# Loading every K and V tile as two column halves, one through the SyncE queue and one through the ScalarE queue

## The chip, the cores and the metric

The kernel runs on one core of one Trainium2 chip. The metric is the time of one execution in microseconds of device time. A time in this document is the median of a kernel's runs. Where a kernel was timed, its runs took turns with runs of the kernel before on the same chip. The kernel before had 1334.65 us (three runs, 1334.62 to 1334.92).

## The reference

The kernel computes one decode step of attention over a long cache, next to a small gated MLP mixer. Only the attention matters here, and of the rest only that it has weights to load.

```python
# B = 2, Sq = 1, D = 1024, H = 32 heads, Sk = 16384, Dh = 128, all bf16
q = (x @ wq).reshape(B, Sq, H, Dh).transpose(0, 2, 1, 3)
scores = einsum("bhqd,bhkd->bhqk", q, k_cache) * (Dh ** -0.5)
p = softmax(scores)
o = einsum("bhqk,bhkd->bhqd", p, v_cache)
a = o.transpose(0, 2, 1, 3).reshape(B, Sq, H * Dh) @ wo
b = mixer(x, w1, w2, w3, w4)             # cut: layernorm, gelu, shifts
return g * a + (1 - g) * b               # g = sigmoid of a row sum
```

The caches hold 2 x 32 heads x 16384 rows x 128 columns x 2 bytes, for K and for V: 537 MB in all. The weights add 36 MB. Every byte is used once, so this is a kernel that reads memory.

## The kernel before

The work is cut into 32 tiles of two heads. One K tile and one V tile are 8 MiB each: 128 partitions with 64 KiB per partition. They are loaded whole, with one transfer each, all from SyncE:

```python
def load_k(i):
    t = big_tile("Kn")                     # one of 3 slots of 64 KiB per partition
    nc.sync.dma_start(out=t[:].rearrange("p (j d) -> p j d", d=Dh),
                      in_=cache_rows(A_k_cache, i))
    kn_tiles[i] = t
# load_v(i): the same; the last V tile alone goes in two halves, both on nc.sync
```

VectorE transposes a K tile in 16 pieces into two T buffers in turn. TensorE makes four score matmuls of each piece, 64 per tile. Because there are two T buffers, a transpose can be at most two pieces ahead of the score matmuls.

```python
def qk_stage(i):
    ...
    for m in range(NM):                    # NM = 16
        T = t_tile([P, 2, CJ, 32], FP32)   # two buffers in turn
        moved = nc.vector.transpose(out=T..., in_=Kw[:, m * CW : (m + 1) * CW]...)
        ...
        for v in range(4):
            nc.tensor.matmul(S[:], lhsT=z[...], rhs=Tb[...], ...)   # scores
```

Then come the softmax (`m`, the maximum; `Pr`, the exponentials on ScalarE; `PT`, their transpose on VectorE) and 64 matmuls `O` with V. The order in which the program asks for all this, and the order of the loads, are these:

```python
for i in range(-1, NT):                                    # NT = 32
    if i + 1 < NT:
        xfers.append(("big", f"k{i + 1}", load K of i + 1))
        steps.append((f"k{i + 1}", scores of i + 1))       # qk_stage
    if i >= 0:
        xfers.append(("big", f"v{i}", load V of i))
        steps.append((f"v{i}", pv_stage(i)))               # O
    if i + 1 < NT:
        steps.append(("", softmax_stage(i + 1)))
    if i in extra:               # after tile 4: w1, w2; after tile 8: w3
        ...
```

The loads go through a ring of three slots in this order: wq, K0, K1, V0, K2, V1 and so on. A load is issued when the slot of the third load before it is free. After V4 the ring takes one slot for w1 and w2, which are 2 MiB each, so only 4 MiB where every other slot takes about 8. From there K6 goes into the slot of K5, and it is issued when the last transpose of K5 is done.

The compile step chooses the order of the instructions on each engine; it may differ from the program's order. Each engine then runs its own list in order. In the kernel before, the compiled order is the program's: no transpose of the next K tile stands inside the softmax of a tile, and all 64 score matmuls of K tile i + 1 stand before the first `O` matmul of tile i.

Of the kernel before, what the change touches and what calls it, by code (L numbers as in the profile page):

```python
# [23 lines left out]
def kernel(  # L24
# [15 lines left out]
    nc = tc.nc  # L40
    P = nc.NUM_PARTITIONS
    B, Sq, D = A_x.shape
    _, H, Sk, Dh = A_k_cache.shape
# [3 lines left out]
    NJ = G * Sk // P  # L47
# [8 lines left out]
    NT = B * NHG  # L56
# [16 lines left out]
    def big_tile(name):  # L73
        return big.tile([P, SLOT], BF16, tag="big", name=name)
# [20 lines left out]
    kn_tiles = {}  # L95
    vn_tiles = {}
    wt = {}
    V_SPLIT_LAST = [NJ // 2, NJ // 2]

    def cache_rows(cache, i):  # L100
        b, hg = tiles[i]
        return cache[b, hg * G : (hg + 1) * G].rearrange("a s d -> (a s) d").rearrange(
            "(p j) d -> p j d", p=P
        )

    def load_k(i):
        t = big_tile("Kn")
        nc.sync.dma_start(
            out=t[:].rearrange("p (j d) -> p j d", d=Dh), in_=cache_rows(A_k_cache, i)
        )  # L110
        kn_tiles[i] = t

    def load_v(i):
        t = big_tile("Vn")
        tv = t[:].rearrange("p (j d) -> p j d", d=Dh)
        src = cache_rows(A_v_cache, i)
        j0 = 0
        for n in V_SPLIT_LAST if i == NT - 1 else [NJ]:
            nc.sync.dma_start(out=tv[:, j0 : j0 + n, :], in_=src[:, j0 : j0 + n, :])
            j0 += n  # L120
        vn_tiles[i] = t



# [55 lines left out]
    def load_first():  # L180
# [12 lines left out]
        out=perm[:].rearrange("k (h a) -> k h a", a=4),  # L193
        in_=ident_f[:].rearrange("k (a h) -> k h a", a=4),
# [28 lines left out]
    for g in range(1, 4):  # L223
        nc.vector.tensor_tensor(
            out=osel_f, in0=osel_f, in1=ident_f[:, 40 * g : 40 * g + 8], op=ALU.add
# [9 lines left out]
        out=pick[:], in_=ident_f[:].rearrange("p (g w) -> p g w", w=32)[:, :, 0:B]  # L235
# [427 lines left out]
    for i in range(-1, NT):  # L663
        if i + 1 < NT:
            xfers.append(("big", f"k{i + 1}", lambda i=i: load_k(i + 1)))
            steps.append((f"k{i + 1}", lambda i=i: (build_z(i + 1), qk_stage(i + 1))))
        if i >= 0:
            xfers.append(("big", f"v{i}", lambda i=i: load_v(i)))
            steps.append((f"v{i}", lambda i=i: pv_stage(i)))
        if i + 1 < NT:  # L670
            steps.append(("", lambda i=i: softmax_stage(i + 1)))
        if i in extra:
            xfers.append(("big", f"x{i}", extra[i][0]))
            steps.append((f"x{i}", extra[i][1]))
# [29 lines left out]
    for b, queue in enumerate((nc.sync, nc.scalar)):  # L704
        queue.dma_start(
            out=out[b].rearrange("s (g n) -> (s g) n", g=NQ), in_=rows[b : 96 + b + 1 : 32, :]
# [31 lines left out]
```

## Time and profile before

| | kernel before |
|---|---|
| time | 1334.65 us |
| span of the profiled run | 1333.3 us |
| queue 1 (SyncE's loads) | 572.53 MB, 99.4% of the time of all 16 DMA engines |
| TensorE, VectorE, ScalarE busy in the span | 806 us, 760 us and 27 us |
| K tile, issue to landing | 51.6 us (median), though 8 MiB move in 19.4 us |

The page of the kernel before says where the time is. The row DMA has one digit per fortieth of the span: 9 is a busy share of 90% or more. The row under it gives the rate in each slice, and the queue line gives packets, megabytes and the share of 16 engines' time.

```profile
span 1333.3 us, 11505 instructions
...
DMA  9999999999999999999999999999999999999998
GB/s 410 439 437 433 423 437 431 427 434 431 439 428 441 431 423 437 441 437 425 433 437 431 433 433 437 433 431 437 435 429 433 437 437 425 435 435 433 431 421 337
...
q1 hardware_dynamic: 12313, 572.53, 99.4%
```

There is no slice in which the loads rest, except at the start and the end. The kernel's time is the time of the packets, 1325 us, plus 8 us. Everything else fits beside it. In the records of the single packets a packet of 64 KB took 2.418 us on one of 16 engines, which is 434 GB/s for all of them. The Trainium skill's page "DMA: Bandwidth & Descriptors" gives a fabric ceiling of 435 GB/s in its Specifications; the trace agrees. (The same table gives about 358 GB/s for one core, which is the 716 GB/s of a stack divided by two cores; this kernel runs on one core, and its trace goes over that figure.)

How much room the compute has is told by what VectorE waits for. The columns of this view are the total wait in us, the number of waits and the longest.

```profile
DVE T L388 <- DMA Kn<-in_A_k_cache_dram: 199.1, 30, 12.1
```

VectorE waits about 6.6 us for each K tile, of the 39 us in which a K tile and a V tile arrive. The list of DMA issues gives the operands, the issuing engine, the count and the median time in us from issue to landing:

```profile
Kn<-in_A_k_cache_dram SPq DMA_DIRECT2D x32, 51.6
```

So in the median a K load is issued 32 us before its turn comes (51.6 less 19.4): one to two tiles stand in the queue in front of it. This time is called the backlog below. For a V load, at 37.2 us in the same list, it is 18 us. That is the slack, in the median. The columns of the timeline are the start, the busy time, engine, line, operation, operands and count; in brackets is the idle time just before and what ended it. `SPq` is SyncE issuing a load.

```profile
217.60 2.37 DVE L388 STREAM_TRANSPOSE T<-Kn 128x1024 f32<-128x1024 f32 x2 [6.77 <-DMA Kn<-in_A_k_cache_dram]
...
222.60 15.64 DVE L388 STREAM_TRANSPOSE T<-Kn 128x1024 f32<-128x1024 f32 x13 [0.46 <-PE S L402]
238.26 0.35 SPq L108 DMA_DIRECT2D Kn<-in_A_k_cache_dram  x1
...
239.28 3.68 PE L446 MATMUL O<-Vn,PT 128*32 128x512 bf16 x64
```

The 16 transposes of K5 took 20.6 us, almost without a break (217.6 to 238.2), then K6 was issued at 238.26, and the stream would have run dry at about 244 (that is where it does run dry in the changed kernel and in e3, which issue K6 later). Here the backlog is about 5.5 us, not 32.

### The profile page before, as it was taken

The numbers are of one execution on the slowest core, as the hardware profiler recorded it, in microseconds if no ns is written. First come the engines' busy times: TensorE is split into PE (matmuls) and PEld (weight loads), VectorE is DVE, ScalarE is ACT, GpSimd is POOL, SyncE is SP. The second block draws the span as 40 slices with busy tenths as digits, with TensorE's granted clock in tenths as the row PEclk, the third lists the DMA queues.
The fourth block names the chain that finished last, engine by engine and source line by source line (L and its number), as shares of the span: only waits on it lengthen the run. The fifth ranks groups of instructions, "written<-read, shape, count | busy, mean of one in ns | idle before, by whom it ended". The sixth has DMA issues, their size and how long they took to land.

```text
span 1333.3 us, 11505 instructions
## 1 busy us (share of the span) xinstructions
PE 805.6 (60%) x4982; PEld 354.5 (27%) x5045; DVE 759.7 (57%) x1001; ACT 27.2 (2%) x68; POOL 12.8 (1%) x40
## 2 busy tenths in 40 slices
PE   2577655766556755556665555566655556665564
PEld 1223222332225322222222222222222222222231
DVE  1677665475652665555666555566655556666540
ACT  0000000000000000000000000000000000000000
POOL 0000000000000000000000000000000000000000
PEclk9788777787777777788887777888777788877775
DMA  9999999999999999999999999999999999999998
GB/s 410 439 437 433 423 437 431 427 434 431 439 428 441 431 423 437 441 437 425 433 437 431 433 433 437 433 431 437 435 429 433 437 437 425 435 435 433 431 421 337
DMA packets 12377, 573.27 MB, mean 430 GB/s; under 512 B 1384, under 2 KB 1392, under 8 KB 2203
## 3 DMA queue, kind: packets, MB, share of 16 engines
q1 hardware_dynamic: 12313, 572.53, 99.4%
q8 instruction: 39, 0.64, 0.2%
q14 instruction: 11, 0.09, 0.0%
q10 hardware_dynamic: 14, 0.01, 0.0%
HBM read 572.53 MB, written 0.00 MB: 429 GB/s over the span
## 4 chain that ended last, share of the span: by engine, by line
PE 31%; DVE 30%; DMA 23%; another core or an unknown queue 12%; issue 2%; ACT 1%; ACTq 0%; SPq 0%; DVEq 0%
DVE T L388 23%; PE S L402 20%; DMA Kn<-in_A_k_cache_dram 13%; PE O L446 7%; DMA wt<-in_B_w_dram 4%; DMA Vn<-in_A_v_cache_dram 3%; DMA wo<-in_A_wo_dram 3%; PE misc L255 2%; DVE Os L461 2%; ACT Pr L430 1%; DVE PT L434 1%; PE misc L604 1%; PE misc L585 1%; DVE mx L423 1%
## 5 line engine op out<-in xcount | busy, mean ns | idle before, releaser
L402 PE MATMUL S<-T,z 128*128 128x512 bf16 x1985 | 583.6, 423 | 323.7 <-DVE T L388 304.5
L388 DVE STREAM_TRANSPOSE T<-Kn 128x1024 f32<-128x1024 f32 x512 | 612.0, 1229 | 252.5 <-DMA Kn<-in_A_k_cache_dram 199.1
L402 PEld LDWEIGHTS <-z 128*128 128x128 bf16 x2048 | 211.2, 104 | 682.8 <-issue 521.5
L446 PE MATMUL O<-Vn,PT 128*32 128x512 bf16 x2048 | 121.4, 390 | 3.3 <-DMA Vn<-in_A_v_cache_dram 3.3
L446 PEld LDWEIGHTS <-PT 128*32 128x32 bf16 x2048 | 74.3, 140 | 49.2 <-issue 20.4
L457 DVE TENSOR_SCALAR Os<-O,xmask 128x128 f32<-128x128 f32 x32 | 11.2, 351 | 101.3 <-PE O L446 101.3
L255 PE MATMUL misc<-rs,ones_f 128*128 128x2 f32 x64 | 17.9, 350 | 79.1 <-DVE rs L477 79.1
L430 ACT ACTIVATE Pr<-S,nb 128x512 bf16<-128x512 f32 x32 | 22.0, 687 | 1198.9 <-DVE nb L425 1161.1
L469 PE MATMUL misc<-asel,Os 128*128 128x2 f32 x64 | 12.4, 264 | 50.9 <-DVE Os L461 50.9
L413 DVE TENSOR_REDUCE m<-S 128x1 f32<-128x512 f32 x32 | 22.1, 692 | 36.9 <-PE S L402 36.9
L434 DVE STREAM_TRANSPOSE PT<-Pr 128x512 bf16<-128x512 bf16 x32 | 22.8, 711 | 28.7 <-ACT Pr L430 28.7
L255 PEld LDWEIGHTS misc<-rs,ones_f 128*128 128x128 f32 x64 | 16.2, 314 | 83.9 <-issue 81.2
L461 DVE SCALAR_TENSOR_TENSOR Os<-O,xmask,Os 128x128 f32<-128x128 f32 x96 | 33.7, 351 | 3.4
L469 PEld LDWEIGHTS misc<-asel,Os 128*128 128x128 f32 x64 | 9.7, 192 | 65.2 <-DVE Os L461 61.0
L255 PE MATMUL misc<-mdiag,ones_f 128*128 128x128 f32 x64 | 15.5, 325 | 17.1 <-DVE mdiag L416 17.1
L423 DVE TENSOR_REDUCE mx<-misc 64x1 f32<-64x64 f32 x64 | 14.2, 222 | 19.1 <-PE misc L255 18.7
L362 POOL TENSOR_TENSOR z<-qsel,own 128x32 bf16<-128x32 bf16 x32 | 10.7, 333 | 1197.9 <-PE S L402 1168.1
L604 PE MATMUL misc<-xn2T,wt 128*128 128x2 bf16 x224 | 14.4, 202 | 8.0 <-DMA wt<-in_B_w_dram 8.0
L481 DVE RECIPROCAL rinv<-misc 128x2 f32<-128x2 f32 x32 | 5.5, 171 | 22.7 <-PE misc L255 22.7
L703 DVE CAST T<-out_acc 128x256 bf16<-128x256 f32 x1 | 0.4, 425 | 29.7 <-PE out_acc L495 29.7
L604 PEld LDWEIGHTS <-wt 128*128 128x128 bf16 x224 | 14.3, 169 | 8.2 <-DMA wt<-in_B_w_dram 8.2
L484 DVE SCALAR_TENSOR_TENSOR OT<-misc,g_bc,rinv 128x2 bf16<-128x2 f32 x32 | 7.0, 220 | 15.6 <-PE misc L469 15.6
(90 smaller groups left out, 122.3 us busy)
## 6 DMA issues: line engine op xcount, KB each, us to landing
Vn<-in_A_v_cache_dram SPq DMA_DIRECT2D x2, 4096.0 KB, 42.8
wt<-in_B_w_dram SPq DMA_DIRECT2D x1, 7168.0 KB
w<-in_B_w_dram SPq DMA_DIRECT2D x4, 1792.0 KB, 31.6
wo<-in_A_wo_dram SPq DMA_DIRECT2D x6, 1024.0 KB, 34.1
wt<-in_B_w_dram SPq DMA_DIRECT2D x1, 2048.0 KB, 37.3
wt<-in_B_w_dram SPq DMA_DIRECT2D x1, 1536.0 KB, 40.9
wo<-in_A_wo_dram SPq DMA_DIRECT2D x2, 512.0 KB, 18.8
wo<-in_A_wo_dram SPq DMA_DIRECT2D x4, 256.0 KB, 13.7
```

The costliest lines, as they stand in the source:

```text
L255: nc.tensor.matmul(ps[:], lhsT=ones_f[:], rhs=src, start=True, stop=True)
L388: moved = nc.vector.transpose(out=T[:].rearrange("p w j s -> p j w s"), in_=Kw[:, m * CW : (m + 1) * CW].rearrange("p (j w e) -> p j w e", ...
L402: nc.tensor.matmul(S[:], lhsT=z[:, v, NM - 1 - m : NM - 1 - m + P], rhs=Tb[:, v // 2, :, v % 2], start=(m == 0 and v == 0), stop=(m == NM ...
L413: nc.vector.reduce_max(out=m[:], in_=S[:], axis=AX.X)
L423: nc.vector.reduce_max(out=mx[pa, :], in_=mall[pa, pa], axis=AX.X)
L430: nc.scalar.activation(out=Pr[:], in_=S[:], func=ACTF.Exp, bias=nb[:], scale=scale, accum_out=rs[:])
L434: nc.vector.transpose(out=PT[:], in_=Pr[:])
L446: nc.tensor.matmul(O[32 * g : 32 * g + 32, :], lhsT=PT[:, m : CJ * 32 : 16], rhs=V[:, j0 : j0 + 4, :], start=(m == 0), stop=(m == NM - 1),)
L461: nc.vector.scalar_tensor_tensor(out=Os[:], in0=Ox, scalar=xmask[:, x : x + 1], in1=Os[:], op0=ALU.mult, op1=ALU.add,)
L469: nc.tensor.matmul(oc[:], lhsT=Os[:], rhs=asel[:], start=True, stop=True)
L585: nc.tensor.matmul(ps[group(g), :], lhsT=actT[rows, r, :], rhs=w[rows, r, g * HW : (g + 1) * HW], start=False, stop=(n == len(slots) - 1), ...
L604: nc.tensor.matmul(ps[:, c, :], lhsT=w[:, r, :].rearrange("k (p c) -> k p c", c=C)[:, :, c], rhs=actT[:, r, :], start=(r == 0), stop=(r == ...
```

## The change

The intent: two queues with two transfers in flight should keep the 16 DMA engines better fed than one, and the issue work would be shared. The diff:

```diff
-    V_SPLIT_LAST = [NJ // 2, NJ // 2]
+    def load_halves(cache, i, name):
+        t = big_tile(name)
+        tv = t[:].rearrange("p (j d) -> p j d", d=Dh)
+        src = cache_rows(cache, i)
+        for half, queue in enumerate((nc.sync, nc.scalar)):
+            j = slice(half * NJ // 2, (half + 1) * NJ // 2)
+            queue.dma_start(out=tv[:, j, :], in_=src[:, j, :])
+        return t
+
     def load_k(i):
-        t = big_tile("Kn")
-        nc.sync.dma_start(
-            out=t[:].rearrange("p (j d) -> p j d", d=Dh), in_=cache_rows(A_k_cache, i)
-        )
-        kn_tiles[i] = t
+        kn_tiles[i] = load_halves(A_k_cache, i, "Kn")
 
     def load_v(i):
-        ... (one transfer; the last V tile in two halves, all on nc.sync)
+        vn_tiles[i] = load_halves(A_v_cache, i, "Vn")
```

A half has the same 128 partitions and 32 KiB of each. The weights stay on SyncE, each in one transfer as before.

The diff does not touch the compute. The compiled order of the compute changes all the same. In 26 of the 32 tiles of the changed kernel 15 to 18 transposes of the following K tiles now stand on VectorE inside the softmax of a tile, between its maximum and `PT`, where before there were none. TensorE's list changes too.

More of the change, by code (lines that the diff above doesn't have):

```diff
@@ L104, in cache_rows @@
         )
-    def load_k(i):
-        t = big_tile("Kn")
-        nc.sync.dma_start(
-            out=t[:].rearrange("p (j d) -> p j d", d=Dh), in_=cache_rows(A_k_cache, i)
-        )
-        kn_tiles[i] = t
-    def load_v(i):
-        t = big_tile("Vn")
-        tv = t[:].rearrange("p (j d) -> p j d", d=Dh)
-        src = cache_rows(A_v_cache, i)
-        j0 = 0
-        for n in V_SPLIT_LAST if i == NT - 1 else [NJ]:
-            nc.sync.dma_start(out=tv[:, j0 : j0 + n, :], in_=src[:, j0 : j0 + n, :])
-            j0 += n
-        vn_tiles[i] = t
+    def load_halves(cache, i, name):
[6 more added lines that the diff above has]
+        return t
+    def load_k(i):
+        kn_tiles[i] = load_halves(A_k_cache, i, "Kn")
+    def load_v(i):
+        vn_tiles[i] = load_halves(A_v_cache, i, "Vn")
     WAYS, QUAD, BASE, MORE = 3, 4, 6, 18
```

## The prediction

> **What bounds the kernel now.** The load stream. The page gives a span of 1333.3 us; its queue table gives queue 1 alone 572.53 MB and 99.4% of the 16 engines' time: 1325 us of packets in flight, 8 us of start, end and gaps. In the trace's packet records the 8192 packets of 64 KB took 2.418 us each (10th and 90th percentile the same): 27.1 GB/s per engine, 434 GB/s for 16. The Trainium skill ("DMA: Bandwidth & Descriptors", Specifications) puts the fabric ceiling at 435 GB/s; the trace agrees. Compute has slack: in the waits view VectorE's K transposes wait 199 us for K to land (30 times, 6.6 us in each 39 us K/V period). The DMA list shows K landing a median 51.6 us after issue although 8 MB move in 19.4 us: the queue holds a backlog of one to two tiles.
>
> **What the change does.**
> 1. Rate: the same page ("Issuing engines are not separate DMA queues") says that DMAs from several engines share the same 16 DMA engines; only issue time is saved. An issue is 0.33 us on SyncE (timeline), hidden by the backlog. No more bandwidth: at most the 8 us of gaps could be won.
> 2. Packets: 32 KB instead of 64. The last V tile's 32 KB packets took 1.213 us; two cost 8 ns more than one of 64 KB. 504 pairs per engine (63 tiles x 8): +4 us, an estimate.
> 3. Balance: wq, w1/w2 and w3 stay on SyncE, so ScalarE's queue runs ahead beside them. At the start K0 completes after wq + K0 + half of K1 (21 MB, about 49 us) instead of 42. Beside w1/w2 and w3 ScalarE can take two halves, so weights land up to 19 us and the next K about 10 us late. Refills are issued later; the backlog of 15 to 24 us should absorb nearly all. I allow 0 to 8 us of drained queue in total.
> 4. Order: compiled, one tile's softmax is interleaved on VectorE and TensorE with the next tile's transposes and score matmuls, where before it filled the time before K landed. About 2.6 us of VectorE work plus hand-offs move behind the wait for K; V's refill is issued some 4 us later. Off the critical path while there is backlog.
> 5. ScalarE: 64 issues stand before the exponentials, but what they wait for (transposes of that K, matmuls of the previous V) is over before the exponential's bias exists. No stall.
> The end is unchanged: w4 and wo come last on SyncE.
>
> **Sum:** 1334.65 + 4 (packets) + 0 to 8 (drains), less some gaps hidden: 1338 us; range 1331 to 1352. Chances: faster by over 2% 0.02, within 2% 0.90, slower by over 2% 0.08.
>
> **What would show it.** Two queues with about half of the K/V bytes each, together about 99% of the engines' span; slices at 425 to 440 GB/s as before, with possible dips near the start, 270 and 440 us; halves landing about as late as whole tiles before; VectorE's wait for K similar or larger; ScalarE's work unchanged and never on the chain for long.
>
> **What would make it wrong.** Interleaved read streams running below 27 GB/s per engine (packets over twice 1.213 us while sharing); larger drains at the weight loads; in-order VectorE waits that tie two tiles together so that refills come after the queue runs dry; or two rings hiding the per-packet cost (then 1327 to 1333).

## The result, and the profile after

The changed kernel took 1345.68 us (four runs, 1345.20 to 1346.22), against 1334.70 us for the kernel before with its run of the same round. The ratio is 1.0082 with a 95% interval of 1.0065 to 1.0100: the same at 2%, and 11 us longer. Ratios here are the mean time of one kernel's runs over that of the other's in the same rounds, so they are not quite the ratio of the medians. Executions over 1.5% slower than the fastest of the same kernel are left out of the means.

The page of the changed kernel, the same lines:

```profile
span 1344.4 us, 11688 instructions
...
DMA  9999999799999999999999999999999999999997
GB/s 406 436 434 428 431 436 430 330 431 436 434 430 428 432 433 428 435 434 433 428 433 437 434 428 430 437 433 429 430 436 435 430 432 432 434 430 434 431 428 326
...
q1 hardware_dynamic: 12169, 304.09, 52.6%
q10 hardware_dynamic: 9230, 268.45, 46.3%
```

Queue 10 is ScalarE's. Half of the cache bytes go through each queue. The rate per slice is what it was, so two queues gain no bandwidth. One slice stands out, the eighth: 330 GB/s and a 7. A slice is 33.6 us, so the eighth runs from 235 to 269 us. Four windows of 5 us through it:

```profile
core 0: us, PE busy (x) PEld busy (x) DVE busy (x) ACT busy (x) POOL busy (x), PEclk, DMA share, GB/s
235.00:240.00 5.00, 2.63 (x14) 0.86 (x15) 0.00 (x0) 0.00 (x0) 0.00 (x0) 0.60 1.00 428
240.00:245.00 5.00, 4.77 (x22) 1.65 (x22) 3.14 (x4) 0.00 (x0) 0.00 (x0) 0.71 0.91 386
245.00:250.00 5.00, 5.00 (x28) 1.55 (x26) 4.62 (x5) 0.00 (x0) 0.00 (x0) 1.00 0.12 51
250.00:255.00 5.00, 4.22 (x39) 1.71 (x39) 2.56 (x4) 0.00 (x0) 0.34 (x1) 1.00 0.62 210
```

From 244 to 253 us almost nothing is read, while VectorE and TensorE are busy: they are the ones being waited for. In the same windows of the kernel before, the stream was full:

```profile
245.00:250.00 5.00, 3.29 (x17) 1.54 (x19) 2.66 (x13) 0.78 (x2) 0.70 (x1) 0.63 1.00 409
```

The timeline of the changed kernel shows what happened in front of this hole. `ACTq` is ScalarE issuing.

```profile
221.11 1.25 DVE L385 STREAM_TRANSPOSE T<-Kn 128x1024 f32<-128x1024 f32 x1 [14.76 <-DMA Kn<-in_A_k_cache_dram]
...
231.52 0.67 DVE L431 STREAM_TRANSPOSE PT<-Pr 128x512 bf16<-128x512 bf16 x1
232.11 2.33 DVE L385 STREAM_TRANSPOSE T<-Kn 128x1024 f32<-128x1024 f32 x2
...
237.37 1.51 PE L443 MATMUL O<-Vn,PT 128*32 128x512 bf16 x11 [4.65 <-DMA Vn<-in_A_v_cache_dram]
...
240.73 1.25 DVE L385 STREAM_TRANSPOSE T<-Kn 128x1024 f32<-128x1024 f32 x1 [6.29 <-PE S L399]
...
245.96 5.39 DVE L385 STREAM_TRANSPOSE T<-Kn 128x1024 f32<-128x1024 f32 x4
251.38 0.35 SPq L111 DMA_DIRECT2D Kn<-in_A_k_cache_dram  x1
251.39 0.36 ACTq L111 DMA_DIRECT2D Kn<-in_A_k_cache_dram  x1
```

Read it from the end. K6 was issued at 251.38, 13 us later than before, because the last transpose of K5 ended then. K5's transposes took 30.3 us (221.1 to 251.4) instead of 20.6. In their midst stands the softmax of tile 4 (`PT` at 231.52). Then TensorE, which works through its list in order, came to `O` of V4 and stood there for 4.65 us until V4 had landed, with the rest of K5's score matmuls behind it. VectorE, at most two T buffers ahead, stood for 6.29 us behind TensorE. So the transposes of K5 waited for V4, a load they have nothing to do with, and K6's load waited for the transposes. K5 itself also came 3.5 us later, 221.1 instead of 217.6, but that mattered little: in e3 below K5 begins at 217.5, and K6 is still issued only at 249.93. What held both was the landing of V4 (TensorE went on at 237.37 here and at 236.79 in e3).

VectorE's waits for K also grew, because its list now has a softmax in it after the wait for K instead of before:

```profile
DVE T L385 <- DMA Kn<-in_A_k_cache_dram: 351.6, 31, 15.8
```

and the halves of K landed 30.8 and 30.1 us after their issue in the median (before: 51.6). This is not the same at every tile. From the issue of a K load to its first transpose it was about 51 us before at most tiles; in the changed kernel it is mostly 43 to 50 us up to K16 and 29 to 31 us from K17 on. So the refills from K17 on are issued some 22 us later, measured against their use, and none of these empties the queue. Only the refill of K5's slot does.

To see how much the hole explains, I summed the packet records of the two load queues: the time of the packets divided by 16 engines ("in flight"), the time in which fewer than 16 packets were in flight ("idle"; an instant with 4 packets counts as 12/16), and the time in which more than 16 were recorded at once, because one packet's record ends a little after the next one's begins ("overlap"). A hole is a stretch in the middle of the run with such idle time, and its size is this average over the 16 engines: of the 7.15 us below, only 3.0 us had no packet in flight at all. In flight plus idle less overlap falls short of the span by 2.5 us in each kernel listed (a gap of 2.5 us at the end, before the result is stored, is left out), so differences can be read from it. These are own sums over the trace, not a view of the profile.

| | in flight, us | idle, us | of it holes | overlap, us | span, us |
|---|---|---|---|---|---|
| before | 1325.0 | 8.5 | none | 2.7 | 1333.3 |
| after | 1330.0 | 16.5 | 7.15 (244 to 253 us) | 4.6 | 1344.4 |
| difference | +5.0 | +8.0 | | -1.9 | +11.1 |

Two parts, then: about 3 us of smaller packets (5.0 less 1.9), and about 8 us of an idle stream, 7.15 of it in one hole. This is a reading. The experiments have to show that the two causes are the right ones.

### The profile page after: what moved, and what is told of

Same layout as the page of the kernel before. It is cut to its first block, busy times and chain, and to the rows that moved or that the text cites. A ratio compares the mean times of both kernels' runs of the same rounds, so it can differ in the third digit from the quotient of the medians.

```text
span 1344.4 us, 11688 instructions
## 1 busy us (share of the span) xinstructions
PE 802.9 (60%) x4978; PEld 342.3 (25%) x5045; DVE 734.7 (55%) x1001; ACT 27.3 (2%) x68; POOL 12.7 (1%) x40
## 4 chain that ended last, share of the span: by engine, by line
DMA 71%; PE 17%; DVE 10%; another core or an unknown queue 1%; issue 1%; DVEq 0%; SPq 0%
DMA Kn<-in_A_k_cache_dram 53%; DMA Vn<-in_A_v_cache_dram 13%; PE O L443 9%; DVE T L385 9%; PE S L399 7%; DMA wo<-in_A_wo_dram 3%; DMA wt<-in_A_wq_dram 2%; PE misc L252 1%; PE misc L327 0%; DVE m L410 0%; DVE Os L458 0%; DVE PT L431 0%; DVE mx L420 0%; DVE T L336 0%
## 5 line engine op out<-in xcount | busy, mean ns | idle before, releaser
L385 DVE STREAM_TRANSPOSE T<-Kn 128x1024 f32<-128x1024 f32 x512 | 622.5, 1236 | 401.3 <-DMA Kn<-in_A_k_cache_dram 351.6
L399 PEld LDWEIGHTS <-z 128*128 128x128 bf16 x2048 | 200.9, 102 | 772.4 <-issue 615.6
L443 PE MATMUL O<-Vn,PT 128*32 128x512 bf16 x2048 | 161.6, 431 | 41.6 <-DMA Vn<-in_A_v_cache_dram 27.9
L443 PEld LDWEIGHTS <-PT 128*32 128x32 bf16 x2048 | 79.1, 144 | 116.5 <-issue 54.2
L327 PE MATMUL misc<-wt,xT 128*2 128x512 bf16 x64 | 5.4, 510 | 18.8 <-DMA wt<-in_A_wq_dram 18.8
L252 PEld LDWEIGHTS misc<-rs,ones_f 128*128 128x128 f32 x64 | 13.3, 251 | 12.2 <-issue 5.4
L252 PE MATMUL misc<-rs,ones_f 128*128 128x2 f32 x64 | 15.0, 305 | 1.9 <-DVE rs L474 1.9
L466 PEld LDWEIGHTS misc<-asel,Os 128*128 128x128 f32 x64 | 13.1, 212 | 11.4 <-DVE Os L458 4.9
L492 PE MATMUL out_acc<-wo,Q 128*2 128x256 bf16 x128 | 8.0, 368 | 9.7 <-DMA wo<-in_A_wo_dram 9.7
## 6 DMA issues: line engine op xcount, KB each, us to landing
Kn<-in_A_k_cache_dram SPq DMA_DIRECT2D x32, 4096.0 KB, 30.8
Kn<-in_A_k_cache_dram ACTq DMA_DIRECT2D x32, 4096.0 KB, 30.1
```

What stands on the lines that cost most here:

```text
L252: nc.tensor.matmul(ps[:], lhsT=ones_f[:], rhs=src, start=True, stop=True)
L385: moved = nc.vector.transpose(out=T[:].rearrange("p w j s -> p j w s"), in_=Kw[:, m * CW : (m + 1) * CW].rearrange("p (j w e) -> p j w e", ...
L399: nc.tensor.matmul(S[:], lhsT=z[:, v, NM - 1 - m : NM - 1 - m + P], rhs=Tb[:, v // 2, :, v % 2], start=(m == 0 and v == 0), stop=(m == NM ...
L443: nc.tensor.matmul(O[32 * g : 32 * g + 32, :], lhsT=PT[:, m : CJ * 32 : 16], rhs=V[:, j0 : j0 + 4, :], start=(m == 0), stop=(m == NM - 1),)
L466: nc.tensor.matmul(oc[:], lhsT=Os[:], rhs=asel[:], start=True, stop=True)
```

## The experiments

The theories:

- **A**: packets of half the size cost about 3 us, and the changed compiled order at K5 makes the hole. The second queue as such costs nothing.
- **B**: two queues disturb each other in the DMA engines.
- **C**: the two queues carry unequal loads. The weights stay on SyncE, a tile is there only when its later half is there, so one queue falls behind and the other runs dry.
- **D**, formed after the first runs: A and C both, the second hidden by the first.

Runs e1 to e4 shared one chip, e5 to e8 a second, e9 and e10 a third; each group has its own runs of the kernel before (medians 1334.71, 1334.80 and 1334.71 us). All kernels gave correct results.

### e1: both halves on one queue

```diff
-        for half, queue in enumerate((nc.sync, nc.scalar)):
+        for half, queue in enumerate((nc.sync, nc.sync)):
```

> Both halves of every tile on SyncE; compiled, VectorE and TensorE keep the order of the kernel before. Theory A (half of the loss is the 32 KB packets, the rest is one hole in the load stream, made by the changed instruction order at K tile 5): packets only, 1338 to 1340.5 us, packets in flight 1329 to 1330 us against 1325 before, no hole between 230 and 260 us. Theory B (the two queues disturb each other): near 1335. Theory C (weights on one queue put the queues out of balance): packets only as in A, 1338 to 1340.5.

Measured: 1337.46 us (1337.38 to 1337.48), ratio 1.0020 (1.0007 to 1.0032), so +2.75 us. Its compiled order is that of the kernel before (one transpose moved, at tile 0). The stream has no hole. The page of e1:

```profile
span 1335.7 us, 11662 instructions
...
q1 hardware_dynamic: 21385, 572.53, 99.5%
```

This is the price of smaller loads by itself. 63 tiles have 16 packets of 32 KB per DMA engine instead of 8 of 64 KB (the last V tile came in halves before), so there are 504 more per engine: 2.75 us / 504 = 5.5 ns for each added packet. Each of the 63 added transfers also ends with a packet of 4 bytes on each engine, and its cost is in that figure; e7 comes back to this. One thing came free: with both halves on one queue the first lands early, and VectorE waits for K only 5.2 us in all (before: 199.1). That wait was slack, so the time has nothing of it.

### e2: two queues, compiled order of before, first try

```diff
+            if m == 0:                          # K's first transpose, every tile
+                tc.keep_in_program_order(moved)
...
+                if m == 0 and g == 0:           # V's first O matmul
+                    tc.keep_in_program_order(mm)
...
-        nc.vector.reciprocal(out=rinv[:], in_=total(rs2[:])[:])
+        nc.vector.reciprocal(out=rinv[:], in_=total(rs2[:], pin=True)[:])
```

> The changed loads exactly, but the next tile's transposes and a V tile's matmuls are pinned to program order, so that VectorE and TensorE run as before. Theory A: no hole near 250 us, 1337 to 1340 us. Theory B: the loss stays, 1344 to 1347. Theory C: w1/w2 are still on SyncE alone, so the hole stays: 1344 to 1347.

Measured: 1342.70 us (1341.38 to 1343.57), ratio 1.0058 (1.0046 to 1.0071). 3 us of the 11 came back. The pin was not tight: one transpose of the next K tile, the second, still slipped ahead of the softmax in VectorE's list at all tiles but 5, 9 and the last. As the list runs in order, that one transpose held up the whole softmax until the next K had landed, and K5's transposes took 27.5 us (219.7 to 247.2). There are holes of 1.1 us at about 100 us and 1.8 us near 245 us. So this run is not a test of the old order; e5 is.

### e3: the loads of before, and only the order of the changed kernel at one tile

This takes the kernel before, with one queue and whole tiles, and mixes V4's matmuls into K5's score matmuls: the first stands after 28 of 64, as in the changed kernel.

```diff
+                if mixed is not None and g == 0 and 3 <= m <= 11:
+                    qk_stage(mixed, m + 4, m + 5)      # a piece of K5 between groups of V4
+                mm = nc.tensor.matmul(O...)
...
+            if i == 4:
+                steps.append(("", scores of 5, pieces 0 to 6))
+                steps.append(("k5", lambda i=i: pv_stage(i, i + 1)))
+                steps.append(("v4", lambda: None))
```

> The loads of the kernel before (one queue, whole tiles); only at tile 5 are V tile 4's matmuls mixed among K tile 5's score matmuls, starting after 28 of 64 as in the changed kernel. Theory A: K tile 5's transposes wait for V tile 4 to land, the refill of its buffer is issued some 10 us later than at 238 us, after the queue ran dry at about 244: a hole of 4 to 8 us, 1338.5 to 1343 us. Theories B and C: nothing of the loads changed, 1334 to 1336.

Measured: 1343.06 us (1342.60 to 1344.31), ratio 1.0064 (1.0050 to 1.0078), so +8.4 us with every load as before. The timeline of e3:

```profile
236.79 1.51 PE L451 MATMUL O<-Vn,PT 128*32 128x512 bf16 x12 [8.10 <-DMA Vn<-in_A_v_cache_dram]
...
240.15 1.25 DVE L389 STREAM_TRANSPOSE T<-Kn 128x1024 f32<-128x1024 f32 x1 [10.19 <-PE S L403]
...
249.93 0.35 SPq L108 DMA_DIRECT2D Kn<-in_A_k_cache_dram  x1
```

and two of its windows, columns as above:

```profile
240.00:245.00 5.00, 5.00 (x30) 1.63 (x30) 4.23 (x4) 0.00 (x0) 0.00 (x0) 0.95 0.84 353
245.00:250.00 5.00, 5.00 (x32) 1.62 (x30) 4.49 (x4) 0.00 (x0) 0.00 (x0) 1.00 0.12 50
```

It is the picture of the changed kernel: TensorE waits for V4 with K5's scores behind it, VectorE waits for TensorE, K6 is issued at 249.93, and the stream has a hole of 6.1 us from 244 to 252. That this order makes the hole is shown: no second queue and no smaller packet is in this kernel. This run is close to a copy of that order at one tile, not an exact one, so its 8.4 us need not be the changed kernel's share to the microsecond.

### e4: the changed kernel, with the weights spread over both queues

```diff
-            nc.sync.dma_start(out=v, in_=src.rearrange("(p r) n -> p r n", p=P))
+            sv = src.rearrange("(p r) n -> p r n", p=P)
+            for half, queue in enumerate((nc.sync, nc.scalar)):
+                r = slice(half * R // 2, (half + 1) * R // 2)
+                queue.dma_start(out=v[:, r, :], in_=sv[:, r, :])   # wq, w1, w3
```

> The changed kernel, with wq, w1 and w3 split over both queues too (order of the engines still interleaved; V tile 4's matmuls start after 40 of tile 5's 64 score matmuls). Theory A: the hole near 250 us stays, smaller or equal, 1341 to 1347 us. Theory C: the queues are balanced, the hole goes, 1337 to 1340. Theory B: 1344 to 1347, without a hole to show for it.

Measured: 1355.92 us (1355.21 to 1357.62), ratio 1.0160 (1.0146 to 1.0174): 10 us slower than the changed kernel, not faster. Under C alone this should have helped. The compiled order changed once more: V4's first matmul stands after 40 score matmuls of K5, V5's after 20 of K6, V9's before any of K10. The holes are at other places now, 8.8 us between 300 and 320 us and 6.7 us between 480 and 500; at 245 only 0.9 us is left. In the trace K6's transposes took 36 us (276.7 to 313.1) and K10's 43 us (450.2 to 493.6). So the balance of the queues was repaired and the order got worse; the run says nothing against C by itself, but it shows how large the order's part can be.

### e5: the changed kernel with the order of before, tight

The pin on the first transpose becomes one on the first two; the other pins are those of e2.

```diff
-            if m == 0:
+            if m <= 1:
                 tc.keep_in_program_order(moved)
```

> The changed loads, with both first transposes of each K tile pinned behind the softmax before them (the run e2 had let one slip through, and it held the whole softmax until K landed). Now the compiled order of VectorE and TensorE is that of the kernel before. Theory A: what one queue of halves cost, 1336.5 to 1339 us, K tile 6 issued before 243 us, no hole over 1 us. Theory B (two queues disturb each other): 1342 to 1347. Theory C (weights on one queue unbalance the two): a hole near 245 us, 1340 or more.

The compiled order is now that of the kernel before at every tile. Measured: 1342.35 us (1340.78 to 1345.16), ratio 1.0059 (1.0047 to 1.0071). The hole at 245 us is gone: K6 was issued at 240.64. But a new hole stands 60 us later. Timeline and windows of e5 (its profiled run is the longest of its five, 1345.16 us, so the hole is probably at its largest here; the other four have no trace):

```profile
240.64 0.35 SPq L111 DMA_DIRECT2D Kn<-in_A_k_cache_dram  x1
240.64 0.36 ACTq L111 DMA_DIRECT2D Kn<-in_A_k_cache_dram  x1
...
289.24 2.37 DVE L387 STREAM_TRANSPOSE T<-Kn 128x1024 f32<-128x1024 f32 x2 [11.87 <-DMA Kn<-in_A_k_cache_dram]
...
309.61 0.33 SPq L111 DMA_DIRECT2D Vn<-in_A_v_cache_dram  x1
```

```profile
245.00:250.00 5.00, 1.63 (x19) 1.01 (x9) 2.98 (x13) 0.63 (x2) 0.00 (x0) 0.91 1.00 428
...
300.00:305.00 5.00, 4.42 (x17) 1.64 (x17) 4.95 (x5) 0.00 (x0) 0.00 (x0) 1.00 0.81 347
305.00:310.00 5.00, 4.23 (x17) 1.64 (x17) 4.53 (x4) 0.00 (x0) 0.00 (x0) 1.00 0.14 59
310.00:315.00 5.00, 4.43 (x70) 2.77 (x67) 1.25 (x4) 0.00 (x0) 0.33 (x1) 1.00 0.95 360
```

The two halves of K6 were issued at the same moment. In the trace's records ScalarE's half landed at 265.4 us and SyncE's at 289.2, 24 us later: SyncE's queue also had w1 and w2 in front of it. SyncE's half is the one that VectorE transposes first, so it could begin K6 only at 289.24, 20 us after the kernel before (269.3). Then V6, which goes into K6's slot, was issued only at 309.61, and the stream had run short from 304 to 311 (5.4 us, counted as in the table above). This is theory C, and it was there all along. In the changed kernel the hole at 245 probably hid it: there, both queues ran empty, which levels them, and K6's halves landed at 274.4 and 274.6.

### e6: halves by partitions instead of by columns

```diff
-            j = slice(half * NJ // 2, (half + 1) * NJ // 2)
-            queue.dma_start(out=tv[:, j, :], in_=src[:, j, :])
+            p = slice(half * P // 2, (half + 1) * P // 2)
+            queue.dma_start(out=tv[p], in_=src[p])
```

> As e5, but the two queues take 64 partitions each instead of half of the columns: packets of 64 KB again, half as many. Theory A: no packet cost and the old order, 1333.5 to 1336 us, about 1325 us of packets in flight. Theory B: over 1338.

The aim was to keep packets of 64 KB with two queues (order pinned as in e5), and so to take the packet cost away. The expectation was a plain miss: the runs took 2501 to 2564 us, median 2542 (three of six slow; the fast ones 2501.32, 2532.17 and 2535.28), ratio of the fast runs 1.8900. The page of e6:

```profile
span 2530.4 us, 11666 instructions
...
DMA packets 13259, 573.28 MB, mean 227 GB/s; under 512 B 2393, under 2 KB 2401, under 8 KB 3212
...
q1 hardware_dynamic: 8073, 304.09, 51.9%
q10 hardware_dynamic: 5134, 268.45, 47.4%
```

The packets are as large as those of before, and their engines are as busy, but a packet of 64 KB took about 4.8 us instead of 2.418 (median of the records). The Trainium skill has this: the page "SBUF — State Buffer", section "Door 1: The DMA port swizzle", gives 64 partitions half of the ports and about 218 GB/s, and the section "Can I just issue two DMAs to hit both halves?" says that two transfers on the two partition halves serialize, measured at 6% over one. The 227 GB/s of this run agree. The run decides nothing between the theories, since it brought in another limit. It costs a factor of nearly two, where the change costs 0.8%.

### e7: quarters on one queue

```diff
-        for half, queue in enumerate((nc.sync, nc.scalar)):
-            j = slice(half * NJ // 2, (half + 1) * NJ // 2)
-            queue.dma_start(out=tv[:, j, :], in_=src[:, j, :])
+        for part in range(4):
+            j = slice(part * NJ // 4, (part + 1) * NJ // 4)
+            nc.sync.dma_start(out=tv[:, j, :], in_=src[:, j, :])
```

> Four quarters of each tile in turn on SyncE, order pinned to that of the kernel before: packets of 16 KB, three more for each one of 64 KB. If each added packet costs the same (e1: 2.75 us for 512 per engine, about 5.4 ns), 1342 to 1344 us, with some 1338 us in flight by the records and a larger overlap. If the cost of e1 was something else (one more issue, one more landing), 1337 to 1340.

Measured: 1343.21 us (1343.03 to 1343.56), ratio 1.0063 (1.0050 to 1.0076), +8.41 us; the order is pinned as in e5, and the stream has no hole. There are 63 x 8 x 3 + 8 x 2 = 1528 more packets per engine: 8.41 us / 1528 = 5.5 ns each, as in e1. So the cost grows in proportion, for halves and for quarters. Whether it is a cost of packets or of transfers the two times can't tell, because both counts grow alike (504 packets with 63 transfers, 1528 with 191), and the other outcome in the expectation was no real alternative: e7 has more issues and landings too. The packet records can tell. From the start of one packet to the start of the next on the same engine, inside a transfer, it takes 2414 ns with 64 KB, 1209 with 32 KB and 607 with 16 KB (medians of before, e1 and e7). Two packets of 32 KB thus cost 4 ns more than one of 64 KB, and four of 16 KB cost 14 ns more, so 4 to 5 ns for each added packet. The 4-byte packet that closes a transfer takes 6 ns. For e1 that gives 504 x 4 + 63 x 6 ns = 2.4 us of the 2.75 measured, most of it the packets.

### e8: the order of before at one tile only

```diff
-            if m <= 1:
+            if i == 5 and m <= 1:               # K5 only; O and rs2 of tile 4 only
```

> The changed kernel, with the old order forced at K tile 5 and V tile 4 alone; elsewhere the softmax stays interleaved with the next tile. Theory A (only the place with little backlog matters): the hole near 245 to 253 us is gone or under 2 us, 1337 to 1341 us, unless it moves to a later tile whose order the compiler changed. If the interleaving costs at every tile: 1343 to 1346 us.

Measured: 1357.69 us (1357.17 to 1358.65), ratio 1.0171 (1.0158 to 1.0185), 12 us slower than the changed kernel. The window of e8 that shows where:

```profile
305.00:315.00 10.00, 9.77 (x122) 4.24 (x122) 8.14 (x13) 0.00 (x0) 0.69 (x1) 1.00 0.05 21
```

The hole at 245 is gone; in its place there is one of 16.5 us, from 303 to 322. Once K5 was pinned, the rest was ordered anew, and V5's first matmul came after only 8 of K6's score matmuls. K6's halves landed 12 us apart (279.7 and 267.4), and K6's transposes took 40.5 us (279.7 to 320.2). The imbalance delayed the start of K6 and the order delayed its end: both at one tile, and the sum is larger than what was repaired.

### e9: order pinned, and the weights balanced

The kernel of e5, with wq, w1, w3 split over both queues as in e4, and the first rows of w2 likewise.

> Two queues of column halves, order pinned as in e5, and wq, w1, most of w2 and w3 split over both queues too. Theory D (the loss has three parts: 32 KB packets, about 2.7 us; the instruction order, which makes a hole near 245 us; and the weights on one queue, which make a hole near 300 us once the order is repaired): only the packets are left, 1336.5 to 1338.5 us, as with one queue of halves (e1: 1337.46), no hole over 1 us, both halves of K tile 6 landed within 5 us of each other. Theory B (a cost of the second queue itself): 1340 or more without a hole.

Measured: 1337.61 us (1337.51 to 1337.86), ratio 1.0022 (1.0008 to 1.0036), +2.9 us. The page, and the two windows that held the hole in e5:

```profile
span 1335.7 us, 11708 instructions
...
q1 hardware_dynamic: 12169, 294.40, 51.2%
q10 hardware_dynamic: 9806, 278.15, 48.3%
```

```profile
300.00:305.00 5.00, 3.47 (x64) 2.08 (x56) 1.92 (x6) 0.00 (x0) 0.22 (x1) 1.00 1.04 442
305.00:310.00 5.00, 0.84 (x4) 0.59 (x4) 1.81 (x7) 0.78 (x2) 0.00 (x0) 0.74 0.99 428
```

(A share can be a little over 1 in a short window, because a packet is put down whole to one window.) No hole is left: 8.3 us idle in the packet sums, nearly all of it at the start and the end. e9 with two queues and e1 with one took the same time within 0.15 us (1337.61 and 1337.46) and have the same span, 1335.7 us. That refutes B: a second queue, with the order and the balance set right, costs nothing beyond the packets. It also gains nothing. The Trainium skill says so on the page "DMA: Bandwidth & Descriptors" ("Issuing engines are not separate DMA queues"): whatever engine issues them, transfers run on the same 16 DMA engines. These runs agree; a 32 KB packet took 1.213 us on one queue, and the same on either while both share.

### e10: order pinned, only w1 and w2 balanced

```diff
-            for half, queue in enumerate((nc.sync, nc.scalar)):
+            for half, queue in enumerate((nc.sync, nc.scalar if key == "w1" else nc.sync)):
```

> As e5, but of the weights only w1 and most of w2 are split over both queues; wq and w3 stay on SyncE. Theory D, if w1/w2 alone put K tile 6's SyncE half 24 us behind its ScalarE half in e5: the hole at 300 us goes, 1336.5 to 1339 us. If the lead that ScalarE has from the start (wq) is what counts: the hole stays, 1340 to 1344.

Measured: 1344.73 us (1343.48 to 1345.39), ratio 1.0073 (1.0060 to 1.0086), slower than e5. The test was to show that w1 and w2 alone make the hole at 300. That hole is indeed gone, but there is one of 4.1 us near 100, as this window shows:

```profile
100.00:105.00 5.00, 4.66 (x33) 2.24 (x35) 3.78 (x5) 0.00 (x0) 0.33 (x1) 1.00 0.32 92
```

The edit had a second effect that I had not seen: wq and w3 stayed on SyncE but became two halves, with packets of 32 KB instead of 64. At the start wq stands on SyncE beside the K halves on ScalarE; K0's first transpose came at 56.5 us (changed kernel 51.8, kernel before 43.2). The packet records show why. While both queues had work, each got about as many packets as the other, so the queue with the larger packets moved more bytes: from 10 to 25 us SyncE's queue moved 4.41 MB and ScalarE's 2.10 in the changed kernel (64 KB against 32 KB), but 3.32 and 3.17 in e10 (32 KB in both). So wq was through at 38.0 us in e10 and at 29.5 in the changed kernel. e10 is therefore confounded and does not separate the weights from each other.

### All runs

| kernel | queues | order | median, us | against before | holes in the stream |
|---|---|---|---|---|---|
| before | 1 | as written | 1334.65 | | none |
| after | 2 | mixed | 1345.68 | +11.0 | 7.15 us at 245 |
| e1 | 1, halves | as written | 1337.46 | +2.75 | none |
| e2 | 2 | one transpose early | 1342.70 | +8.0 | 1.1 at 100, 1.8 at 245 |
| e3 | 1, whole tiles | mixed at K5 | 1343.06 | +8.4 | 6.1 at 245 |
| e4 | 2, weights balanced | mixed anew | 1355.92 | +21.2 | 8.8 at 310, 6.7 at 490 |
| e5 | 2 | as written | 1342.35 | +7.6 | 5.4 at 305 |
| e6 | 2, by partitions | as written | 2542.39 | x 1.89 | not a matter of holes |
| e7 | 1, quarters | as written | 1343.21 | +8.4 | none |
| e8 | 2 | as written at K5 only | 1357.69 | +22.9 | 16.5 at 310 |
| e9 | 2, weights balanced | as written | 1337.61 | +2.9 | none |
| e10 | 2, w1 and w2 balanced | as written | 1344.73 | +10.0 | 4.1 at 100 |

No version beats the kernel before. The best with two queues, e9, is 2.9 us slower than it, and those 2.9 us are the packets.

## Why the prediction was right or wrong

The time was right: 1345.68 us lies in the range of 1331 to 1352, and "within 2%" was the likeliest class. It is 7.7 us above the 1338 that were predicted, about the size of the one hole. That it still falls inside the range is partly luck: the sum allowed 0 to 8 us of drained queue for the weights on one queue (step 3), and the kernel lost 7 us of drained queue for another reason (step 4).

**What bounds the kernel: right.** The load stream bounds both kernels. Each lost microsecond of the stream in the tables above is a microsecond of time.

**Step 1, no more bandwidth: right.** 428 to 437 GB/s in the slices (before: 423 to 441), except for the first and last ones and the eighth. e9 against e1 shows it most cleanly.

**Step 2, packets: right in mechanism, a little too large.** The estimate was +4 us from the record durations (8 ns for each pair); e1 measured 2.75 us, 5.5 ns for each added packet, and e7 the same 5.5 ns. The records of two packets in a row on an engine overlap by about 4 ns (a packet of 32 KB is recorded with 1213 ns, and the next one starts after 1209), so a sum of durations overstates: a pair costs 4 ns more and not 8.

**Step 3, balance: the mechanism exists, but it was not what made the changed kernel's hole.** "Beside w1/w2 and w3 ScalarE can take two halves" did not come true there at 245 us, since K6's halves were not issued until 251.4. The start came nearly as expected: K0 at 51.8 us, where the prediction said about 49. This start also explains why K5 came 3.5 us late. Of the weights only wq is loaded before K5; in every run with two queues of column halves and wq on SyncE alone K5's transposes began at 219.7 to 222.9 us, and with wq on both queues (e4 and e9) at 215.2. The imbalance shows in e5 (K6's halves 24 us apart, a hole at 300 us), and e9 takes it away: 1342.35 against 1337.61 us, 4.7 us, within the predicted 0 to 8.

**Step 4, order: this is the step that failed.** The prediction saw from the compiled order that softmax and transposes would be mixed, and said "V's refill is issued some 4 us later. Off the critical path while there is backlog." Two numbers in it were wrong for the place that counted. The step thought of V's refill; at K5 the refill of the K slot, K6, was issued 13 us later, because TensorE's list had V4's matmuls in the middle of K5's scores and so chained K5's transposes to the landing of V4. And the backlog there was about 5.5 us, not "15 to 24": the slot of w1 and w2 holds 4 MiB instead of 8, and K6 goes into K5's own slot. "Refills are issued later; the backlog of 15 to 24 us should absorb nearly all" was true of every other tile of the changed kernel. e3 shows that this order alone makes such a hole with the old loads, and e5 that it goes when the order is put back. Among the things that "would make the prediction wrong", "in-order VectorE waits that tie two tiles together so that refills come after the queue runs dry" named it, with TensorE as the engine where the tie begins.

**Step 5, ScalarE: right.** Its busy time is 27.3 us against 27.2, and it is not on the chain. The reverse, a load that stands behind an exponential for some time, happened at one tile: V5's ScalarE half was issued at 258.61, 4.3 us after SyncE's half, just behind the exponential that began at 258.51. It cost nothing that the trace shows.

**Signs in the profile.** Right: two queues with about half of the cache bytes each, 98.9% of the engines' time together; VectorE's wait for K larger (199 to 352 us). Wrong: "halves landing about as late as whole tiles before" (30.8 us after issue instead of 51.6); and of the possible dips at the start, 270 and 440 us, only one came, at 244 to 253.

What is shown, and what is not: the 2.75 us of the smaller loads and the cause of the hole are shown. About 1 us of the 11 is neither in the packets nor in the hole and is not accounted for. That the hole at 245 levelled the queues and so spared the changed kernel the hole at 300 is read from the landings in two traces; no run tests it alone.

## What to carry to other kernels

A kernel whose stream is full gains nothing from a second queue, and it pays for smaller packets; a second queue also has to be given equal work, down to the weights, or the later half of a tile sets the pace. Compare the compiled order on every engine and not only the diff, and judge slack at the place where the backlog is smallest, not by its median: 7 us were lost at one tile of 32. And repair all the parts at once before judging one: with the order or the balance repaired alone, at one tile or at all, the time went to 1342, 1356 and 1358 us, and only both together gave 1337.6.

## What the Trainium skill lacked or had wrong

- "DMA: Bandwidth & Descriptors", section "Why small descriptors are slow (HBM only)", names a fixed overhead of about 3 cycles for each packet, but gives no measured time for large packets on a stream that is already full. Here an added packet cost 5.5 ns on its engine, for packets of 32 KB and of 16 KB alike (e1: 2.75 us for 504; e7: 8.41 us for 1528), its share of the transfer's closing packet included.
- "DMA: Bandwidth & Descriptors", section "Issuing engines are not separate DMA queues", is right that only issue time is saved. It does not say what a second queue can cost: with the other loads left on one queue, the two halves of a tile landed 24 us apart, and that cost 4.7 us (e5 against e9).
- The same page's Specifications give about 358 GB/s for one core, a stack's 716 GB/s divided by two cores. Read as a limit for a single core the row misleads: this one-core kernel read 429 GB/s over the whole span, and 434 in full flight. The page is not wrong here, since it says itself, below its table of measured transfers, that the 358 hold with both cores streaming; only the row lacks the condition. The 435 GB/s of the fabric agree.
- "SBUF — State Buffer", section "Can I just issue two DMAs to hit both halves?", was right and would have saved a run: 227 GB/s with two queues on two partition halves. It gives rates only; the run shows a 64 KB packet at about 4.8 us instead of 2.418.
